# Reordering the opening of a windowed-attention and SwiGLU kernel: group 0's values between group 1's keys and queries, and a held first gate unit

## The chip, the cores and the metric

The kernel runs on one core of a Trainium2 chip. The metric is device time in microseconds (us), the median of several executions; lower is better. The engines of a core work side by side, each through its own list of instructions in order: TensorE (PE, matmuls, with its weight loads as PEld), VectorE (DVE), ScalarE (ACT), GpSimd (POOL, which here mostly issues the loads) and SyncE (SP, which issues the stores and the transposing transfers). They wait for each other through semaphores.

## The reference

Attention over 4 batches, 8 heads, 768 positions and head size 64. Each query sees the 128 latest keys up to itself, and the first 4 keys (the sinks). The outputs of the 8 heads stand side by side as one row of 512 per token, and go through a SwiGLU block without biases:

```
scores = scale * q @ k.T ; keep = is_sink | in_window
a = softmax(where(keep, scores, -1e9)) ; attn = a @ v
x = attn.transpose(0, 2, 1, 3).reshape(B * S, H * D)      # 3072 x 512
g = x @ w_gate ; val = x @ w_val                           # 512 x 1536 each
out = (g * sigmoid(g) * val) @ w_out                       # 1536 x 512
```

Inputs and outputs are float32; the kernel works in bfloat16 with float32 sums.

## The kernel before

The 3072 tokens are cut into 12 groups of 256 (three to a batch, `NG`), and attention is done group by group. The block is done in token tiles (`SIZES`): tiles 0, 1 and 2 of 256 tokens are groups 0, 1 and 2; larger tiles follow. The order of all work is written out by hand (`tc.manual_schedule()`): each engine gets its instructions in the order in which the Python code calls them, and nothing is moved by a scheduler.

The steps of attention, each with its line:

- `load_rows` (L95), `load_nat` (L104), `load_v` (L116), `load_gate` (L128), `load_out` (L137) issue loads on POOL's queue. Each issue there takes POOL's time, and POOL's queue lands them in the order of their issue. Keys and queries of group 1 come as `rows`, in two halves each of keys and of queries; the values of a group come as `va`, two halves.
- `step_T` (L220) turns keys or queries of group 1 so that the head size lies on the partitions: 16 matmuls of 64x64 for a half (`p2`) into one bank of PSUM, then one cast to `kT` or `qT` (L235). `step_TN` (L239) does it for later groups from another layout, with 4 transposes.
- `step_S` (L277): scores of 4 heads, 12 matmuls into 4 banks (L292), 4 exps on ACT (L299), and two mask products on DVE (L304). The masks are not issued there but appended to the list `later`; `flush` (L210) issues what the list holds.
- `step_ks` (L262), `step_K` (L308) and `step_vsb` (L268) make the sinks' keys, scores (`pk`, `es`) and values (`vsb`, made on POOL from `diag_h`, which three small DVE rows L602 to L604 compute).
- `step_PV` (L338): values of 4 heads of 128 tokens. In groups other than a batch's first, the first call starts all four `o` banks with the sinks (L335). Then a reciprocal (L363) and the scaled `xn`: by DVE in one row (L369), through `later`, or, with `norm` "a", by ACT in four rows (L366), at once.
- `step_X` (L379): four transposes of `xn` into the `px` bank (L396) and one copy to `xT`, the block's input, by ACT (L399) or DVE (L403), the latter through `later` or at once (`evict` "now").

A unit of the block is `gate` (L448): `gate_a` has `project` (L411) make the gate half `pg` in one bank, and ACT its tanh `th` (L432); then come the unit's attention steps; then `gate_b` makes the value half `pv`, and DVE gates in two rows, `u` (L438) and `ht` (L444). For a 256-token tile each half is 8 matmuls of 128x256. `both` (L455) does two units as gate half, gate half, value half, value half. `down` (L462) multiplies by `w_out`, scales and stores.

All PSUM tiles come from one pool of 8 banks, `bank` (L78), used in turn: a tile waits until the tile eight before it has been read.

The opening: group 0 comes pair by pair (`pair_T`, `pair_S`, `pair_mask`). L614 to L633 then interleave group 1's turning, group 0's values, transposes and group 1's scores. From L640 the list `us` holds the units in their order, and `weave` (L513) calls them, each with the attention steps that the slots (L654) give to its place: place 0 is unit (0, 0) of tile 0, place 1 is unit (0, 2) with group 1's values between its halves, place 2 is group 1's transposes alone, place 3 is units (0, 4) and (1, 0) through `both`, places 4 and 5 are units (1, 2) and (1, 4) with the turning of group 2. From place 6 on the units cover tiles 0 and 1 together, 512 tokens wide.

Of the kernel before, what the change touches and what calls it, by code (L numbers as in the profile page):

```python
# [14 lines left out]
def kernel(  # L15
# [12 lines left out]
    nc = tc.nc  # L28
# [55 lines left out]
    def by_rows(src, b, w, pairs, t0):  # L84

        hs = slice(2 * pairs.start + w, 2 * pairs.stop, 2)
        return src[b, hs, t0:t0 + 256].rearrange("p (m r) d -> m p (r d)", r=4)
# [3 lines left out]
    def new_rows(g):  # L91
        rows[g] = rowp.tile([P, 2, NP2, 4 * D], BF16, tag="rows", name="rows")
        return rows[g]

    def load_rows(g):  # L95
        b, c = divmod(g, GC)
        x = new_rows(g)
        for i in range(2):
            for w in range(2):
                nc.gpsimd.dma_start(  # L100
                    x[64 * w:64 * (w + 1), i],
                    by_rows((k, q)[i], b, w, ALL, c * 256))

    def load_nat(g):  # L104
        b, c = divmod(g, GC)
# [10 lines left out]
    def load_v(g):  # L116
        b, c = divmod(g, GC)
        va = vpool.tile([P, 2, H, VS], BF16, tag=f"va{g}", name="va")
        nc.vector.memset(va[:, :, :, D:D + 1], 1.0)  # L119
        for j in range(2):  # L120
            t0 = c * 256 + j * P
            nc.gpsimd.dma_start(  # L122
                va[:, j, :, 0:D], v[b, :, t0:t0 + P].rearrange("h p d -> p h d"))
        vas[g] = va
# [62 lines left out]
    for i in range(2):  # L187
# [2 lines left out]
                   allow_small_or_imprecise_dtypes=True)  # L190
    nc.gpsimd.iota(tk, [[0, 1]], base=0, channel_multiplier=1,
                   allow_small_or_imprecise_dtypes=True)
    load_rows(1)
    load_v(0)
    nc.gpsimd.iota(th8, [[-32, 4], [-NS, 4]], base=0, channel_multiplier=1,
                   allow_small_or_imprecise_dtypes=True)
    load_gate(0)
# [12 lines left out]
    def flush():  # L210
        for f in later:
            f()
        later.clear()
# [48 lines left out]
    def step_ks(b):  # L262
        for h in range(2):
            r = slice(h * D, (h + 1) * D)
            (nc.vector.tensor_copy if b else nc.scalar.copy)(
                out=kss[r, b, :, h * NS:(h + 1) * NS], in_=kTs[b][r, :, 0:NS])
# [144 lines left out]
    def project(ws, tb, f, name):  # L411
        n = xTs[tb].shape[2]
        ps = bank([P, 512], FP32, name)
        for i in range(512 // n):
            fi, fo = FOF[f + i]
            for c in range(DMC):
                nc.tensor.matmul(  # L417
                    ps[:, i * n:(i + 1) * n], ws[fi][:, c, fo * P:(fo + 1) * P],
                    xTs[tb][:, c], start=(c == 0), stop=(c == DMC - 1))
        return ps  # L420

    def gate_a(tb, f):
        if tb not in hts:
            n = SIZES[tb]
            t = hpool.tile([P, DFC * 512], BF16, tag="ht", name="ht")
            hts[tb] = dense(t, DFC, n)
            if tb == 0:
                hts["01"] = t.rearrange("p (b c n) -> p b c n", b=2, c=DFC)
                hts[1] = t[:, DFC * n:2 * DFC * n].rearrange("p (c n) -> p c n", c=DFC)
        pg = project(wgs, tb, f, "pg")  # L430
        th = tpool.tile([P, 512], FP32, tag="th", name="th")
        nc.scalar.activation(th, pg, AF.Tanh, scale=0.5)  # L432
        return pg, th

    def gate_b(tb, f, pg, th):
        pv = project(wvs, tb, f, "pv")
        u = upool.tile([P, 512], BF16, tag="u", name="u")
        nc.vector.scalar_tensor_tensor(u, th, 1.0, pg, op0=ALU.add, op1=ALU.mult)  # L438
        if tb == "01":
            nc.vector.tensor_tensor(  # L440
                hts[tb][:, :, f], *(x.rearrange("p (b n) -> p b n", b=2) for x in (u, pv)),
                op=ALU.mult)
            return
        nc.vector.tensor_tensor(  # L444
            hts[tb][:, f:f + 512 // SIZES[tb]].rearrange("p a n -> p (a n)"), u, pv,
            op=ALU.mult)
# [5 lines left out]
        gate_b(tb, f, *a)  # L452
        flush()

    def both(one_, two_, attn):  # L455

        a = [gate_a(*x) for x in (one_, two_)]
        for x, y in zip((one_, two_), a):
            gate_b(*x, *y)
        flush()  # L460

    def down(tb, ts, attn, last=False):  # L462
        at = {}
# [5 lines left out]
        for m, (lo, hi) in enumerate(parts):  # L469
# [11 lines left out]
            else:  # L481
                nc.vector.tensor_scalar(ot, po, 0.5, None, op0=ALU.mult)  # L482
            nc.sync.dma_start(out[r0:r0 + P, lo:hi], ot)

    def alone(tb, f, attn):
        pro(*attn)
        flush()

    def gates(tb):
        return [(gate, tb, f) for f in range(0, DFC, 512 // SIZES[tb])]  # L490
# [4 lines left out]
    def A(fn, *a):  # L495
        return lambda: fn(*a)

    def TN(g, evict="av"):
        return [A(step_TN, g, i, j, evict) for j in range(2) for i in range(2)]

    def Ss(g):
        return [A(step_S, g, p2) for p2 in range(2)]
# [7 lines left out]
    def K(g):  # L510
        return A(step_K, g)

    def weave(us, slots):  # L513
        assert all(i < len(us) for i in slots)
        for i, (fn, tb, x) in enumerate(us):
            fn(tb, x, slots.get(i, []))

    def pro(*steps):
        for s in steps:
            s()  # L520
            if len(later) > 1:
                later.pop(0)()

    def slots(*pairs):
        sl = {}
# [49 lines left out]
    def pair_mask(p):  # L575
        e = e_t[0][:, 2 * p:2 * p + 2, P:512]
        m = mask0.rearrange("q (o a) x -> q o (a x)", o=1)[:, :, P:512]
        nc.vector.tensor_tensor(e, e, m.broadcast_to([P, 2, 384]), op=ALU.mult)
# [20 lines left out]
    pair_S(3, 2)  # L599
    for p in range(1, NP2):  # L600
        pair_mask(p)
    nc.vector.tensor_scalar(lt8, th8, float(NS), None, op0=ALU.is_lt)  # L602
    nc.vector.scalar_tensor_tensor(lt8, th8, 0.0, lt8, op0=ALU.is_ge, op1=ALU.mult)
    nc.vector.tensor_reduce(diag_h, lt8.rearrange("p q h -> p h q"), mybir.AxisListType.X,  # L604
# [6 lines left out]
    load_gate(5)  # L611
    for i in range(4):
        load_out(i)
    step_T(1, 0, 0, "a")  # L614
    step_T(1, 0, 1, "a")
    step_T(1, 1, 0, "a")
    step_PV(0, 0, 0)
    step_PV(0, 0, 1)
    flush()
    step_T(1, 1, 1, "a")  # L620
    step_ks(0)
    step_PV(0, 1, 0)
    step_PV(0, 1, 1)
    flush()
    step_S(1, 0)
    masks1 = list(later)
    later.clear()
    step_X(0, 0)
    step_X(0, 1)
    flush()  # L630
    step_S(1, 1)
    later[:0] = masks1
    flush()  # L633
    load_nat(3)
    load_v(3)
    nc.gpsimd.memset(vcl, 0.0)
# [1 line left out]
    load_sinks(vcl, 1, B)  # L638

    g0, g1, g2 = gates(0), gates(1), gates(2)  # L640
    us = [g0[0], g0[1], (alone, 0, 0), (both, g0[2][1:], g1[0][1:]), g1[1],
          g1[2], *((gate, "01", f) for f in range(6, DFC)),
          *g2, *downs(0), *downs(1), *downs(2)]

    def L(*fs):
# [5 lines left out]
    def NV(g):  # L651
        return L(A(load_nat, g), A(load_v, g))

    weave(us, slots(  # L654
        (0, [K(1)]), (1, [A(step_PV, 1, 0, 0), A(step_PV, 1, 0, 1, "a"), A(step_PV, 1, 1, 0),
                              A(step_PV, 1, 1, 1, "a"), flush]),
        (2, [A(step_X, 1, 0, "a"), A(step_X, 1, 1, "now")]),
        ((4, 4, 5, 5), TN(2)), ((6, 7), Ss(2)), (6, [K(2)]),
        ((8, 8), PVs(2)[:2]), (9, [A(step_PV, 2, 0, 1, "a"), A(step_PV, 2, 1, 1, "a")]),
        ((10, 11), [A(step_X, 2, 0, "a"), A(step_X, 2, 1, "a")]),  # L660
        (11, [NV(4), lambda: nc.gpsimd.tensor_copy(out=vcl[64:128], in_=vcl[0:64])]), ((14, 14, 15, 15), TN(3, "aa")),
        (15, [A(xbar, 4)]), (15, [NV(5)]), (19, [A(xbar, 5)]), (19, [NV(6)]),
        (23, [A(xbar, 6)]), (23, [NV(7)]),
        ((17, 18), Ss(3)), (18, [A(step_ks, 1)]), (18, [A(step_vsb, 1)]),
# [59 lines left out]
```

## Time and profile before

| what | before |
|---|---|
| median of 4 runs | 239.22 us (238.61 to 239.97) |
| the profiled execution | 238.98 us, of which the span from first to last instruction is 237.2 us |
| granted TensorE clock, mean over the span | 0.999 |
| busy PE / DVE / ACT / POOL | 231.3 / 158.2 / 114.6 / 74.5 us |
| first gate half (`pg`) starts | 14.89 us |
| first 512-wide unit starts | 29.46 us |

All times within a profile are microseconds from the start of the span. A row of the timeline gives start, length, engine, line, operation, output and inputs, shapes, number of instructions, and in square brackets the idle time of the engine before it with what ended it. A length runs from the first start to the last end of the merged instructions, so that rows of a pipelined engine overlap by about 0.2 us on PE. A wait for several semaphores is put down to the one that came last. The digits of the 40 slices are tenths of busy share. The issue rows of POOL tell when a load is issued, not when its data land; landings are told separately.

In the stretch from 9 to 23 us the other engines' rows that matter for the change are these (start, length; engine, line and output; number):

```profile
12.35 0.59 ACT L235 CAST qT<-pt 128x512 bf16<-128x512 f32 x1 [0.73 <-PE pt L230]
12.83 0.41 ACT L265 COPY kss<-kT 64x16 bf16<-64x16 bf16 x2
13.27 4.03 ACT L299 ACTIVATE e<-s 128x512 bf16<-128x512 f32 x8
...
19.54 1.75 ACT L366 ACTIVATE xn<-o,rcp 128x64 bf16<-128x64 f32 x8 [0.90 <-DVE rcp L363]
21.13 0.64 ACT L399 COPY xT<-px 128x512 bf16<-128x512 bf16 x1
```

### The profile page before, as it was taken

Reading aid. Unit: us, or ns where it says so; the run is one execution under the profiler, and the core shown is the slowest. Engines: PE = TensorE matmul, PEld = TensorE weight load, DVE = VectorE, ACT = ScalarE, POOL = GpSimd, SP = SyncE. Lnnn points to the kernel's source line nnn. Section 1 sums busy time; section 2 is a strip of 40 time slices with the busy share of each in tenths; the row PEclk is TensorE's granted clock in tenths of the full one; section 3 lists DMA queues with packets and bytes.
Section 4 is the critical chain, followed back from the end, with each engine's and each line's share of the span. In section 5 each row is a group of like instructions: output and inputs, shape, how many; then the busy total and the mean of one; then the engine's idle time right before and its main releaser. Section 6 shows DMA issues by size and latency. Waiting matters only on the chain.

```text
span 237.2 us, 4913 instructions
## 1 busy us (share of the span) xinstructions
PE 231.3 (98%) x1901; PEld 127.7 (54%) x1901; DVE 158.2 (67%) x335; ACT 114.6 (48%) x237; POOL 74.5 (31%) x98
## 2 busy tenths in 40 slices
PE   8899999999999999999999999999999999999994
PEld 5577845795554444544444444444444445488443
DVE  5888778768652888960798980688970598877000
ACT  4896485467452836512845622655622663333221
POOL 8996875713508026170261700080000000000000
PEclk9999999999999999999999999999999999999999
DMA  8999999994999959999499994599214100200132
GB/s 139 157 182 177 181 200 205 157 148 75 158 170 153 164 107 118 143 121 220 112 115 123 109 79 147 137 88 140 44 21 140 63 3 0 44 3 1 52 128 88
DMA packets 107655, 27.36 MB, mean 115 GB/s; under 512 B 94704, under 2 KB 104688, under 8 KB 107632
## 3 DMA queue, kind: packets, MB, share of 16 engines
q0 software_dynamic: 76640, 13.90, 74.9%
q1 hardware_dynamic: 30448, 12.89, 25.4%
q8 instruction: 15, 0.25, 0.4%
q10 hardware_dynamic: 544, 0.26, 0.4%
q14 instruction: 8, 0.07, 0.1%
HBM read 28.34 MB, written 6.29 MB: 146 GB/s over the span
## 4 chain that ended last, share of the span: by engine, by line
PE 89%; ACT 4%; DVE 2%; DMA 2%; issue 1%; POOL 0%; DVEq 0%; ACTq 0%; POOLq 0%
PE pd L475 26%; PE pv L417 26%; PE pg L417 25%; PE o L355 4%; PE s L292 4%; DMA x<-in_q_dram 2%; ACT e L299 2%; PE pn L245 1%; ACT xn L366 1%; ACT e L572 1%; PE o L335 1%; ACT th L432 1%; PE pk L320 1%; DVE u L438 1%; PE px L396 0%
## 5 line engine op out<-in xcount | busy, mean ns | idle before, releaser
L438 DVE SCALAR_TENSOR_TENSOR u<-th,pg 128x512 bf16<-128x512 f32 x72 | 49.1, 683 | 38.9 <-ACT th L432 38.9
L417 PE MATMUL pv<-xT,wv 128*128 128x512 bf16 (+1 forms) x360 | 74.1, 337 | 0.3 <-ACT e L299 0.2
L417 PE MATMUL pg<-xT,wg 128*128 128x512 bf16 (+1 forms) x360 | 74.1, 336 | 0.2
L432 ACT ACTIVATE th<-pg 128x512 f32<-128x512 f32 x72 | 43.5, 604 | 62.3 <-PE pg L417 61.7
L475 PE MATMUL pd<-wo,ht 128*128 128x512 bf16 (+2 forms) x300 | 65.7, 371 | 0.0
L444 DVE TENSOR_TENSOR ht<-u,pv 128x512 bf16<-128x512 bf16 x66 | 45.4, 688 | 10.4 <-PE pv L417 4.5
L417 PEld LDWEIGHTS <-wg 128*128 128x128 bf16 x360 | 35.0, 98 | 28.1 <-issue 0.7
L299 ACT ACTIVATE e<-s 128x512 bf16<-128x512 f32 (+1 forms) x88 | 42.7, 581 | 3.5 <-PE s L292 3.5
L475 PEld LDWEIGHTS <-ht 128*128 128x128 bf16 x300 | 27.9, 98 | 30.0 <-issue 0.5
L417 PEld LDWEIGHTS <-wv 128*128 128x128 bf16 x360 | 32.0, 98 | 20.7 <-issue 1.6
L111 POOL DMA_DIRECT2D nat<-in_k_dram x20 | 17.6, 887 | 75.9 <-DMA qT<-nat 73.9
L480 ACT ACTIVATE ot<-pd 128x512 f32<-128x512 f32 (+1 forms) x24 | 14.3, 596 | 47.4 <-PE pd L475 47.4
L304 DVE TENSOR_TENSOR e<-e,mask 128x1024 bf16<-128x1024 bf16 (+1 forms) x44 | 27.2, 652 | 4.2 <-ACT e L299 4.2
L122 POOL DMA_DIRECT2D va<-in_v_dram x24 | 21.5, 917 | 4.7 <-DMA wo<-in_moe_w_out_dram 2.5
L369 DVE TENSOR_TENSOR xn<-o,rcp 128x256 bf16<-128x256 f32 x44 | 18.7, 424 | 1.5
L355 PEld LDWEIGHTS <-e 128*128 128x128 bf16 x352 | 15.0, 98 | 8.0 <-DVE va L119 0.5
L111 POOL DMA_DIRECT2D nat<-in_q_dram x20 | 17.7, 896 | 1.1 <-DMA wv<-in_moe_w_val_dram 0.5
L355 PE MATMUL o<-va,e 128*128 128x65 bf16 x352 | 17.0, 193 | 0.3 <-DVE va L119 0.3
L292 PE MATMUL s<-qT,kT 64*128 64x128 bf16 (+1 forms) x240 | 12.9, 237 | 0.0
L292 PEld LDWEIGHTS <-kT 64*128 64x128 bf16 x240 | 7.7, 94 | 7.6 <-issue 6.6
L482 DVE TENSOR_SCALAR ot<-pd 128x128 f32<-128x128 f32 x1 | 0.3, 292 | 14.3 <-PE pd L475 14.3
L363 DVE RECIPROCAL rcp<-o 128x4 f32<-128x4 f32 x48 | 8.1, 174 | 1.6 <-PE o L355 1.4
(73 smaller groups left out, 93.3 us busy)
## 6 DMA issues: line engine op xcount, KB each, us to landing
out_dram<-ot SPq DMA_DIRECT2D x23, 256.0 KB
va<-in_v_dram POOLq DMA_DIRECT2D x24, 128.0 KB, 6.5
nat<-in_k_dram POOLq DMA_DIRECT2D x20, 128.0 KB, 4.9
nat<-in_q_dram POOLq DMA_DIRECT2D x20, 128.0 KB, 5.8
wg<-in_moe_w_gate_dram POOLq DMA_DIRECT2D x6, 256.0 KB, 7.8
wv<-in_moe_w_val_dram POOLq DMA_DIRECT2D x6, 256.0 KB, 8.1
wo<-in_moe_w_out_dram POOLq DMA_DIRECT2D x4, 384.0 KB, 10.9
st<-in_q_dram ACTq DMA_DIRECT2D x2, 128.0 KB
```

Of the source, the lines that this page charges most:

```text
L111: nc.gpsimd.dma_start(x[:, i, j].rearrange("p (h d) -> p h d", d=D), src[b, :, t0:t0 + P].rearrange("h p d -> p h d"))
L122: nc.gpsimd.dma_start(va[:, j, :, 0:D], v[b, :, t0:t0 + P].rearrange("h p d -> p h d"))
L292: nc.tensor.matmul(pss[2 * pp + h][:, col:col + n], kTs[b][r, p, kk:kk + P], qTs[b][r, p, qq:qq + n], start=True, stop=True)
L299: nc.scalar.activation(e_t[g][:, h0 + h, lo:512], pss[2 * pp + h][:, lo:512], AF.Exp, scale=scale)
L304: nc.vector.tensor_tensor(e, e, m[:, :, lo:512].broadcast_to([P, 2, 512 - lo]), op=ALU.mult)
L355: nc.tensor.matmul(o, l, r, start=(c == 0 and i == 0), stop=(i == len(mms) - 1), skip_group_check=True)
L369: nc.vector.tensor_tensor(xn, po[:, :, 0:D], rcp.broadcast_to([P, 4, D]), op=ALU.mult)
L417: nc.tensor.matmul(ps[:, i * n:(i + 1) * n], ws[fi][:, c, fo * P:(fo + 1) * P], xTs[tb][:, c], start=(c == 0), stop=(c == DMC - 1))
L432: nc.scalar.activation(th, pg, AF.Tanh, scale=0.5)
L438: nc.vector.scalar_tensor_tensor(u, th, 1.0, pg, op0=ALU.add, op1=ALU.mult)
L444: nc.vector.tensor_tensor(hts[tb][:, f:f + 512 // SIZES[tb]].rearrange("p a n -> p (a n)"), u, pv, op=ALU.mult)
L475: nc.tensor.matmul(po, hts[tb][:, f, ts * P:(ts + 1) * P], wos[f // n][:, f % n, lo:hi], start=(f == 0), stop=(f == DFC - 1))
```

## The change

Loads: `load_rows` takes the tensor as an argument (0 keys, 1 queries), and group 0's values are issued between group 1's keys and queries instead of behind them. The three DVE rows for `diag_h`, `step_vsb` and the loads behind it are called after group 0's transposes instead of before group 1's turning.

Opening: group 1's keys are turned; then group 0's values (heads 4 to 7 of its first 128 tokens scaled by ACT); then group 1's queries; then the sinks' keys, transposes of group 0's first 128 tokens, scores (1, 0), transposes of the second 128 tokens. Both copies to `xT` are issued at once on DVE.

Units: `both`, `alone` and `pro` go. `gate_held` is unit (0, 0): gate half, then `step_K(1)`, scores (1, 1) and all four masks of group 1, then the value half; its tanh and gating rows are not issued but held. `gate_first` is unit (0, 2): gate half, group 1's values (heads 0 to 3 of both halves by ACT, heads 4 to 7 by DVE), the held tanh, its own tanh, transposes (1, 0), its value half, transposes (1, 1), then the gating of both units. Then the order is (1, 0), (1, 2), (0, 4), (1, 4); group 2's two key steps stand in place 4 and its two query steps in place 5.

```
@@ -92,14 +92,14 @@
...
 
-    def load_rows(g):
-        b, c = divmod(g, GC)
-        x = new_rows(g)
-        for i in range(2):
-            for w in range(2):
-                nc.gpsimd.dma_start(
-                    x[64 * w:64 * (w + 1), i],
-                    by_rows((k, q)[i], b, w, ALL, c * 256))
+    def load_rows(g, i):
+        b, c = divmod(g, GC)
+        if g not in rows:
+            new_rows(g)
+        for w in range(2):
+            nc.gpsimd.dma_start(
+                rows[g][64 * w:64 * (w + 1), i],
+                by_rows((k, q)[i], b, w, ALL, c * 256))
 
...
@@ -190,8 +190,9 @@
...
                    allow_small_or_imprecise_dtypes=True)
-    load_rows(1)
+    load_rows(1, 0)
     load_v(0)
+    load_rows(1, 1)
     nc.gpsimd.iota(th8, [[-32, 4], [-NS, 4]], base=0, channel_multiplier=1,
...
@@ -420,6 +421,10 @@
...
     def gate_a(tb, f):
+        new_h(tb)
+        return tanh(project(wgs, tb, f, "pg"))
+
+    def new_h(tb):
         if tb not in hts:
...
@@ -427,13 +432,16 @@
...
                 hts[1] = t[:, DFC * n:2 * DFC * n].rearrange("p (c n) -> p c n", c=DFC)
-        pg = project(wgs, tb, f, "pg")
+
+    def tanh(pg):
         th = tpool.tile([P, 512], FP32, tag="th", name="th")
...
     def gate_b(tb, f, pg, th):
-        pv = project(wvs, tb, f, "pv")
+        gate_v(tb, f, pg, th, project(wvs, tb, f, "pv"))
+
+    def gate_v(tb, f, pg, th, pv):
         u = upool.tile([P, 512], BF16, tag="u", name="u")
...
@@ -452,12 +460,31 @@
...
 
-    def both(one_, two_, attn):
-
-        a = [gate_a(*x) for x in (one_, two_)]
-        for x, y in zip((one_, two_), a):
-            gate_b(*x, *y)
+    held = []
+
+    def gate_held(tb, f, attn):
+
+        new_h(tb)
+        pg = project(wgs, tb, f, "pg")
+        for step in attn:
+            step()
+        pv = project(wvs, tb, f, "pv")
+        held.extend([lambda: held.append(A(gate_v, tb, f, *tanh(pg), pv))])
+
+    def gate_first(tb, f, attn):
+
+        pg = project(wgs, tb, f, "pg")
+        for hh, norm in ((0, "a"), (1, "v")):
+            for j in range(2):
+                step_PV(1, j, hh, norm)
         flush()
+        held.pop(0)()
+        a = tanh(pg)
+        step_X(1, 0, "now")
+        pv = project(wvs, tb, f, "pv")
+        step_X(1, 1, "now")
+        held.pop(0)()
+        gate_v(tb, f, *a, pv)
 
...
@@ -482,10 +509,6 @@
...
 
-    def alone(tb, f, attn):
-        pro(*attn)
-        flush()
-
     def gates(tb):
...
@@ -514,12 +537,6 @@
...
             fn(tb, x, slots.get(i, []))
-
-    def pro(*steps):
-        for s in steps:
-            s()
-            if len(later) > 1:
-                later.pop(0)()
 
...
@@ -599,6 +616,20 @@
...
         pair_mask(p)
+    step_T(1, 0, 0, "a")
+    step_T(1, 0, 1, "a")
+    step_PV(0, 0, 0)
+    flush()
+    step_PV(0, 0, 1, "a")
+    step_PV(0, 1, 0)
+    step_PV(0, 1, 1)
+    flush()
+    step_T(1, 1, 0, "a")
+    step_T(1, 1, 1, "a")
+    step_ks(0)
+    step_X(0, 0, "now")
+    step_S(1, 0)
+    step_X(0, 1, "now")
     nc.vector.tensor_scalar(lt8, th8, float(NS), None, op0=ALU.is_lt)
...
@@ -611,26 +642,6 @@
...
         load_out(i)
-    step_T(1, 0, 0, "a")
-    step_T(1, 0, 1, "a")
-    step_T(1, 1, 0, "a")
-    step_PV(0, 0, 0)
-    step_PV(0, 0, 1)
-    flush()
-    step_T(1, 1, 1, "a")
-    step_ks(0)
-    step_PV(0, 1, 0)
-    step_PV(0, 1, 1)
-    flush()
-    step_S(1, 0)
-    masks1 = list(later)
-    later.clear()
-    step_X(0, 0)
-    step_X(0, 1)
-    flush()
-    step_S(1, 1)
-    later[:0] = masks1
-    flush()
     load_nat(3)
...
@@ -638,8 +649,8 @@
...
     g0, g1, g2 = gates(0), gates(1), gates(2)
-    us = [g0[0], g0[1], (alone, 0, 0), (both, g0[2][1:], g1[0][1:]), g1[1],
-          g1[2], *((gate, "01", f) for f in range(6, DFC)),
+    us = [(gate_held, *g0[0][1:]), (gate_first, *g0[1][1:]), g1[0], g1[1], g0[2], g1[2],
+          *((gate, "01", f) for f in range(6, DFC)),
           *g2, *downs(0), *downs(1), *downs(2)]
...
@@ -652,13 +663,12 @@
...
     weave(us, slots(
-        (0, [K(1)]), (1, [A(step_PV, 1, 0, 0), A(step_PV, 1, 0, 1, "a"), A(step_PV, 1, 1, 0),
-                              A(step_PV, 1, 1, 1, "a"), flush]),
-        (2, [A(step_X, 1, 0, "a"), A(step_X, 1, 1, "now")]),
-        ((4, 4, 5, 5), TN(2)), ((6, 7), Ss(2)), (6, [K(2)]),
+        (0, [K(1), A(step_S, 1, 1), flush]),
+        (4, TN(2)[::2]), (5, TN(2)[1::2]), ((6, 7), Ss(2)), (6, [K(2)]),
         ((8, 8), PVs(2)[:2]), (9, [A(step_PV, 2, 0, 1, "a"), A(step_PV, 2, 1, 1, "a")]),
         ((10, 11), [A(step_X, 2, 0, "a"), A(step_X, 2, 1, "a")]),
-        (11, [NV(4), lambda: nc.gpsimd.tensor_copy(out=vcl[64:128], in_=vcl[0:64])]), ((14, 14, 15, 15), TN(3, "aa")),
+        (11, [NV(4), lambda: nc.gpsimd.tensor_copy(out=vcl[64:128], in_=vcl[0:64])]),
+        ((14, 14, 15, 15), TN(3, "aa")),
         (15, [A(xbar, 4)]), (15, [NV(5)]), (19, [A(xbar, 5)]), (19, [NV(6)]),
...
```

## The prediction

> **What bounds the kernel now.** I read the page first: the engines' shares and the 40 slices.
>
> ```profile
> PE 231.3 (98%) x1901; PEld 127.7 (54%) x1901; DVE 158.2 (67%) x335; ACT 114.6 (48%) x237; POOL 74.5 (31%) x98
> ...
> PE   8899999999999999999999999999999999999994
> ...
> PEclk9999999999999999999999999999999999999999
> ```
>
> TensorE (PE) is the bound and has 5.9 us without work in a span of 237.2. Next, busy time by stretches, to see where those 5.9 us lie (columns: stretch, its length, then busy us of each engine with its instructions, the granted clock, DMA share, GB/s).
>
> ```profile
> 10.00:20.00 10.00, 9.16 (x163) 7.02 (x162) 8.68 (x26) 8.06 (x20) 9.45 (x13) 1.00 1.67 181
> ...
> 30.00:60.00 30.00, 29.87 (x274) 19.11 (x272) 23.52 (x47) 19.33 (x44) 15.18 (x21) 1.00 1.55 156
> 60.00:100.00 40.00, 39.90 (x341) 19.65 (x340) 28.36 (x61) 20.60 (x42) 13.15 (x16) 1.00 1.40 146
> ...
> 150.00:200.00 50.00, 50.00 (x366) 23.86 (x365) 36.55 (x70) 24.30 (x49) 5.25 (x6) 1.00 0.51 71
> ```
>
> From 30 us on PE never lacks work for long, so a delay made in the opening is carried to the end, and a gain too. The edit changes no arithmetic: it can only close or open holes on PE before 30 us. So I read PE's rows of the opening in order of time (start, length, group, idle time before it and what ended that).
>
> ```profile
> 8.80 1.24 PE L230 MATMUL pt<-ident,rows 64*64 64x64 bf16 x33
> 10.37 0.63 PE L230 MATMUL pt<-ident,rows 64*64 64x64 bf16 x15 [0.32 <-DMA rows<-in_q_dram]
> 11.34 0.40 PE L355 MATMUL o<-va,e 128*128 128x65 bf16 x8 [0.34 <-DVE va L119]
> ...
> 14.89 1.03 PE L417 MATMUL pg<-xT,wg 128*128 128x256 bf16 x8
> ...
> 20.25 0.92 PE L396 MATMUL px<-ident,xn 128*128 128x128 bf16 x7
> 21.35 0.23 PE L396 MATMUL px<-ident,xn 128*128 128x128 bf16 x1 [0.18 <-ACT xn L366]
> ...
> 21.42 2.07 PE L417 MATMUL pg<-xT,wg 128*128 128x256 bf16 x16
> ```
>
> What to see: PE waits for group 1's query rows at 10.37, for group 0's values at 11.34 (the row names a memset on VectorE, but it ends at 11.31 by chance; the values' first half had landed at 11.20). At 21.42 one row holds 16 matmuls: 8 are unit (0,4)'s gate half, which needs nothing new, and only the next 8, from 22.45, need group 1's turned output. Work stands ready where the last copy of xT is waited for.
>
> The loads that set the first two waits, on GpSimd's (POOL's) queue:
>
> ```profile
> 4.47 1.27 POOL L100 DMA_DIRECT2D rows<-in_q_dram  x2
> 5.68 1.85 POOL L122 DMA_DIRECT2D va<-in_v_dram  x2
> ```
>
> The landing marks give key rows 8.27 and 8.92, query rows 9.59 and 10.32, values 11.20 and 11.99: half a row load adds 0.65 to 0.73 us to the line, half a value load 0.79 to 0.88.
>
> **The change, part by part.** The order is fixed by hand, so what the new source says is what each engine gets. I walk it forward from 8.80 us: an instruction starts when its engine is free and what it waits for has ended, about 0.05 us later on PE and 0.03 elsewhere. Prices, start to start, from rows of the opening: 8 matmuls of a gate half 0.875 us; 16 of a turn of rows 0.48; 12 of scores 0.44; 8 value matmuls 0.24; 4 transposes 0.22; about 0.1 where PE changes its tile shape; about 0.2 from a matmul's start to its result. ScalarE: cast 0.59, exp 0.48 apart, scaling of one head 0.2 apart. VectorE: reciprocal 0.17, xn 0.42, copy of xT 0.42, mask 0.69, the three lt/diag rows with the memsets together 0.8.
>
> 1. *Values before query rows on POOL's queue.* By the steps above, after 8.92 the values land at 9.8 and 10.6, the queries at 11.3 and 12.05. Bounds for the second query half: 10.3 if the value packets cost the queue nothing, 12.6 if a value half takes 5.5 us from issue (as in this trace) and the queries queue up behind both. I take 12.05, since the total moved up to then was 11.99 before. SP's queue and the later loads keep their order.
>
> 2. *Group 0's values between keys and queries.* Keys end on PE at 9.9. Heads 0 to 3 go at 10.0, heads 4 to 7 at 10.52 (the last mask ends at 10.48), the other 16 matmuls from 10.65 to 11.1. Before, they ended at 12.7. Moving part of xn to ScalarE (11.16 to 12.11) costs nothing: ScalarE would wait for the queries there. But PE then waits until 12.1 for the queries, turns them until 13.1, and transposes xn's first half at 13.13. The first scores need the first query cast (12.80 to 13.39), so they run 13.45 to 13.95. The second half of xn goes at 14.02, its copy runs 14.48 to 14.91, and the first gate half starts at 14.96. Before it started at 14.89. The earlier values win nothing there, because the chain query rows, cast, scores, second transpose, copy runs from the delayed landing.
>
> 3. *Scores (1,1) behind the first gate half.* At 14.89 the kernel before had both score sets of group 1 done; now the second set follows at 16.10 to 16.54, so 0.44 plus two shape changes, some 0.6 us, are still owed. It waits on no bank: its four wait for a copy and three exps that end by 15.5.
>
> 4. *Held unit, values behind the second gate half.* PE runs without a hole from 14.96 to 20.0: gate half, sinks' scores 15.93, scores, value half to 17.50, second gate half to 18.37, sinks 18.46, 32 value matmuls 18.8 to 20.0. ScalarE's last exp ends at 18.57, the last mask at 19.29, when PE reaches its heads at about 19.3: just covered, and a late exp is paid one to one. Then reciprocals 19.24 onward and ScalarE's eight scalings from 19.45 to 21.23. VectorE's xn of heads 4 to 7 end at 20.36 and 20.91. Transposes (1,0) finish at 20.6 (0.35 us of hole), the value half fills 20.66 to 21.54, transposes (1,1) go right behind. The held tanh is queued on ScalarE behind the scalings and both gating pairs on VectorE behind the copies; who waits for them is PE, for banks, at 26.9, when the bank has been free since 23.8: nothing.
>
> 5. *Unit (1,0) directly after.* The copy of transposes (1,1) runs 22.00 to 22.43, and PE stands from 21.77 to 22.48: here the old order had unit (0,4)'s gate half as cover, and the new one has none. Unit (1,0) starts at 22.48 against 22.45 in the trace, but with one gate half, 0.875 us, less behind it.
>
> 6. *Group 2's keys in one unit, queries in the next; lt8 rows after the xT copies.* The same transposes in other pairs: nothing. vsb moves from 14.28 to 15.7 and the group-2 loads, issued behind it, from 14.85 to about 16.3; they stand in a queue whose line lands them at 23.2 and later, and PE wants the keys at 26.9 and the queries at 29.1: nothing, at worst (1.4 us later, 26.8) still nothing.
>
> The sum: from 22.48, eight gate or value halves (7.0) and 16 transposes (0.89) reach the first 512-wide unit at 30.36. The same count for before, seven halves from 22.45, gives 29.46, which is what the trace has. So +0.9 us. The profiled execution took 238.98 (span 237.2 and 1.8 around it), and the sum is 239.9 on it; that execution lies 0.24 below the median 239.22, so for a median I say 240.1: slower by 0.4%, within the 0.5% (1.2 us) that this kernel's runs can tell from no change.
>
> **A rule weighed.** Row first: PEclk is 9 in every slice, and the 14 filling matmuls at the start lie 0.21 us apart where a gate half's, equally wide, lie 0.109 apart later. The Trainium skill ("TensorE: Matmul & The Clock Gate", Part 1) says that the clock falls to half after an idle window of about 3.4 us. It speaks against holes such as the new one at 11.1 to 12.1, but by its figure no hole of the walk is long enough and the sum stays; were it to fall, my estimate from the page is 1.7 us for one window.
>
> **Rivals.**
> - *Not slower: the swap costs the queries nothing.* If they land by about 11 us, item 2's chain starts at the end of the values, the first gate half at 14.1, and 0.85 of the 0.9 us is won back: 239.2. For it: transfers of one queue overlap in flight (issue to landing 5.1 us against 0.6 us between landings). Against: six landings one behind the other, at the pace of their sizes. It decides once the second half lands before 11.1.
> - *Later queries or masks.* Landing at 12.6 puts 0.55 on top, the exps late by 0.3 another 0.3: 240.6 to 241.0. For it: item 4 has no slack; against: the walk over the old order came out 0.05 to 0.1 us from the trace.
> - *The clock.* With PE thinner from 10 to 12 us a slow stretch as at the start (matmuls at twice the distance for the 3.7 us between the first filling matmul and 4.75, where the record of the clock begins) would cost 1.85: 242.0. Against: before idles 0.6 and 0.5 us in the same stretch at full clock.
>
> **How the numbers follow.** The walk 0.63 (own range 239.6 to 240.7), queries not late 0.12, later 0.17, clock 0.05, something faster that I do not see 0.03. The range runs from 238.9 (queries not late, less the runs' scatter) to 241.4 (later ones, plus it). Slower by over 0.5% means above 240.4: a third of the walk, most of the later ones, the clock: 0.40. Faster by over 0.5%: 0.03. The rest, 0.57, lies within.
>
> **What the next profile would show.** Values on PE at 10.0 and a wait there for query rows ending near 12.1; first gate half near 15.0; scores between the first gate half and its value half; PE idle some 0.7 us before unit (1,0), released by the copy of xT; the first 512-wide unit near 30.4 against 29.46. The prediction is wrong if the query rows land near 10.5, if PE's hole before unit (1,0) is short, or if the stretch from 30 us to the end changes its length.

## The result and the profile after

The changed kernel takes 240.01 us in the median (239.37 to 241.65 in 38 executions) against 239.31 us for the kernel before, run beside it: a ratio of 1.0028 with a 95% interval of 1.0017 to 1.0038, so 0.4 to 0.9 us slower, 0.67 in the middle (the medians lie 0.70 apart). The profiled execution took 239.67 us with a span of 237.9 (before: 238.98 and 237.2). I read it in the order in which the prediction read the profile before. First the page: busy time of the engines, the slices and the granted clock.

```profile
PE 231.0 (97%) x1901; PEld 127.8 (54%) x1901; DVE 158.0 (66%) x335; ACT 114.9 (48%) x240; POOL 74.9 (31%) x98
...
PE   7898999999999999999999999999999999999994
...
PEclk9999999999999999999999999999999999999999
```

The work is the same, the clock is the same, and TensorE (PE) has 6.9 us without work where it had 5.9. Then busy time by stretches (stretch, its length, busy us of PE, PEld, DVE, ACT and POOL with their instructions, granted clock, DMA share, GB/s).

```profile
10.00:20.00 10.00, 9.02 (x177) 7.06 (x171) 7.52 (x25) 8.78 (x25) 8.76 (x12) 1.00 1.56 176
20.00:25.00 5.00, 4.30 (x42) 3.68 (x42) 4.23 (x10) 2.65 (x9) 3.67 (x5) 1.00 2.12 169
...
30.00:60.00 30.00, 29.87 (x271) 19.19 (x270) 23.75 (x45) 19.27 (x44) 15.45 (x21) 1.00 1.54 156
...
150.00:200.00 50.00, 50.00 (x368) 23.82 (x367) 35.96 (x69) 24.73 (x50) 5.25 (x6) 1.00 0.52 72
```

From 30 us on, PE's busy time is that of before to the hundredth in these stretches (29.87 and 50.00): what was lost was lost earlier. The stretch from 20 to 25 us has 4.30 busy where the kernel before had 4.82:

```profile
20.00:25.00 5.00, 4.82 (x44) 3.71 (x43) 3.54 (x8) 2.96 (x10) 3.17 (x5) 1.00 2.11 168
```

PE's rows of the opening show where (start, length, group, and in brackets the idle time before it with what ended it).

```profile
9.46 1.08 PE L231 MATMUL pt<-ident,rows 64*64 64x64 bf16 x32
10.48 0.35 PE L356 MATMUL o<-va,e 128*128 128x65 bf16 x6
11.20 0.72 PE L356 MATMUL o<-va,e 128*128 128x65 bf16 x18 [0.36 <-DVE e L595]
11.85 1.23 PE L231 MATMUL pt<-ident,rows 64*64 64x64 bf16 x32
...
14.80 1.03 PE L418 MATMUL pg<-xT,wg 128*128 128x256 bf16 x8 [0.52 <-DVE xT L404]
...
15.99 0.61 PE L293 MATMUL s<-qT,kT 64*128 64x128 bf16 x12
...
20.32 0.34 PE L397 MATMUL px<-ident,xn 128*128 128x128 bf16 x3 [0.18 <-ACT xn L367]
20.50 1.04 PE L418 MATMUL pv<-xT,wv 128*128 128x256 bf16 x8
21.37 0.39 PE L397 MATMUL px<-ident,xn 128*128 128x128 bf16 x4
22.27 1.03 PE L418 MATMUL pg<-xT,wg 128*128 128x256 bf16 x8 [0.52 <-DVE xT L404]
...
30.15 1.03 PE L418 MATMUL pg<-xT,wg 128*128 128x512 bf16 x4
```

Two holes of 0.52 us are new, both ended by a copy to xT (L404): one ahead of the first gate half, one ahead of unit (1, 0) at 22.27. Before, a single row of 16 gate matmuls stood over the second. The first 512-wide unit starts at 30.15 against 29.46, 0.69 later, which is the difference of the two spans. That an opening's loss arrives whole at the end holds for nearly every profile of this study: from the first 512-wide unit to the end of the span it is 207.74 to 207.78 us in twelve of the thirteen, and 209.12 in one of the better versions below. The list of PE's waits between 7 and 32 us sums it up (line, waited for, us in total, times, longest):

```profile
PE pg L418 <- DVE xT L404: 1.0, 2, 0.5
PE o L356 <- DVE e L595: 0.4, 1, 0.4
```

Two more of 0.2 each follow. The same list of the kernel before has four waits of 0.3, 0.3, 0.2 and 0.2, some 1.0 us in all against 1.8 here; its two longest are those for the values and for the query rows, as the prediction read them:

```profile
PE o L355 <- DVE va L119: 0.3, 1, 0.3
PE pt L230 <- DMA rows<-in_q_dram: 0.3, 1, 0.3
```

In this profile of the changed kernel the waits for loads are gone, and waits for VectorE came in their place. The loads of POOL's queue:

```profile
3.23 1.28 POOL L100 DMA_DIRECT2D rows<-in_k_dram  x2
4.47 1.83 POOL L122 DMA_DIRECT2D va<-in_v_dram  x2
6.29 1.26 POOL L100 DMA_DIRECT2D rows<-in_q_dram  x2
```

Their landing marks are 9.24 and 10.24 for the values, 11.07 and 11.95 for the queries (predicted 9.8, 10.6, 11.3, 12.05). PE does not show a wait for the queries in this execution, because group 0's staged loads landed late (ScalarE waited for the last of them until 5.62; before, until 4.65), the keys' turn began at 9.46 instead of 8.80, and PE came to the queries only at 11.85. That start is not the change's doing: over all the profiles of this study it lies between 8.60 and 9.71 us, whatever the kernel (last section).

### The profile page after: what moved, and what is told of

The parts are those of the page before. It is cut to its first block, busy times and chain, and to the rows that moved or that the text cites. A ratio compares the mean times of both kernels' runs of the same rounds, so it can differ in the third digit from the quotient of the medians.

```text
span 237.9 us, 4912 instructions
## 1 busy us (share of the span) xinstructions
PE 231.0 (97%) x1901; PEld 127.8 (54%) x1901; DVE 158.0 (66%) x335; ACT 114.9 (48%) x240; POOL 74.9 (31%) x98
## 4 chain that ended last, share of the span: by engine, by line
PE 90%; ACT 3%; DVE 2%; DMA 2%; issue 1%; ACTq 0%; DVEq 0%
PE pd L502 26%; PE pv L418 26%; PE pg L418 26%; PE s L293 4%; PE o L356 4%; DMA st<-in_q_dram 2%; ACT e L300 1%; PE px L397 1%; PE pn L246 1%; ACT e L589 1%; PE pk L321 1%; PE o L336 1%; ACT th L438 1%; PE pt L231 0%; ACT xn L367 0%
## 5 line engine op out<-in xcount | busy, mean ns | idle before, releaser
L502 PEld LDWEIGHTS <-ht 128*128 128x128 bf16 x300 | 27.9, 98 | 29.9 <-issue 0.5
L370 DVE TENSOR_TENSOR xn<-o,rcp 128x256 bf16<-128x256 f32 x43 | 18.2, 424 | 1.5
## 6 DMA issues: line engine op xcount, KB each, us to landing
wo<-in_moe_w_out_dram POOLq DMA_DIRECT2D x4, 384.0 KB, 11.1
```

The lines of the kernel that those rows point to most:

```text
L370: nc.vector.tensor_tensor(xn, po[:, :, 0:D], rcp.broadcast_to([P, 4, D]), op=ALU.mult)
L502: nc.tensor.matmul(po, hts[tb][:, f, ts * P:(ts + 1) * P], wos[f // n][:, f % n, lo:hi], start=(f == 0), stop=(f == DFC - 1))
```

## The experiments

The theory: unit (1, 0) has lost its cover, the gate half of unit (0, 4), and that is the main loss. The rivals: the later landing of the query rows is the main loss; the held tanh and gating rows are. Each of the kernels below computes the whole reference. Since the start of an opening wanders, I use two measures beside the ratio: the time from the last of the six loads (key rows, query rows, values) to the first 512-wide unit, and the time from group 0's first transposes (px), or the first gate half, to that unit.

**The cover put back.** Unit (0, 4) goes through `both` with (1, 0) again; all else as after.

```
-    us = [(gate_held, ...), (gate_first, ...), g1[0], g1[1], g0[2], g1[2],
+    us = [(gate_held, ...), (gate_first, ...), (nothing, 0, 0),
+          (both, g0[2][1:], g1[0][1:]), g1[1], g1[2],
```

> The changed kernel with one thing put back: unit (0,4)'s gate half stands again between group 1's last transposes and unit (1,0)'s gate half (the two units as gate half, gate half, value half, value half). Theory A (the walk on record: the loss is the missing cover for the last copy of xT): the hole before unit (1,0), 0.5 us in the profile of the changed kernel, is filled, the first 512-wide unit starts at 29.5 to 29.6 instead of 30.15, time about 239.4 to 239.5, ratio to before 1.000 to 1.001. Rival B (the loss is the later landing of the query rows): it stays at 30.1, ratio 1.003. Rival C (the loss is the held gating, crowding VectorE and ScalarE behind the copies): it stays at 30.1 or a wait for a bank shows up, ratio 1.003 or more.

Measured: 239.30 us against 239.14, ratio 1.0006 [0.9983, 1.0030]. PE's rows:

```profile
14.25 1.03 PE L418 MATMUL pg<-xT,wg 128*128 128x256 bf16 x8 [0.52 <-DVE xT L404]
...
20.96 0.39 PE L397 MATMUL px<-ident,xn 128*128 128x128 bf16 x4
21.31 1.92 PE L418 MATMUL pg<-xT,wg 128*128 128x256 bf16 x16
23.54 1.92 PE L418 MATMUL pv<-xT,wv 128*128 128x256 bf16 x16 [0.31 <-DMA wv<-in_moe_w_val_dram]
...
29.68 1.03 PE L418 MATMUL pg<-xT,wg 128*128 128x512 bf16 x4
```

The hole before unit (1, 0) is gone: from the second transposes (px) to the next gate half it is 0.35 us (20.96 to 21.31) where it was 0.90 (21.37 to 22.27), and from the first gate half to unit (1, 0)'s place it is 7.06 us instead of 7.47. But the covering unit needs the third chunk of `wv`, which lands at 23.49, and PE now stands there: the values begin 0.48 us after the 16 gate matmuls would have ended (21.31 plus two halves of 0.875 is 23.06). From the first gate half to the wide unit it is 15.43 us against 15.35 after, so in this execution the gain was paid back. Measured against the kernel before, the time is 0.5 us better than the whole change's, with intervals that overlap. The cover is a real part of the loss; this run alone does not give its size.

**The old load order, the rest as after.**

```
-    load_v(0)
     load_rows(1, 1)
+    load_v(0)
```

> The changed kernel with the loads in the old order (group 1's queries issued ahead of group 0's values), PE's order unchanged. A: the queries still stand behind the values on PE, and the values now land near 12.0, so everything behind shifts by 0.5 to 0.6 us: first gate half at 15.3 to 15.5, first 512-wide unit at 30.7 to 30.8, ratio 1.005 to 1.006. B: the queries land at 10.3 again and the loss goes: 29.5, ratio 1.000. C: as the changed kernel, 1.003.

Measured: 240.15 us against 239.14, 1.0041 [1.0021, 1.0062]. The queries landed at 9.03 and 10.03, and the first 512-wide unit came at 30.33 (I expected 30.7 to 30.8). This profile cannot judge the loads: as in the first one of after, PE shows no wait for a load in its opening, and the unit's 0.18 us go with a start of the keys' turn that was 0.25 later (9.71). The times can: taking the swap back wins nothing, so the later landing of the query rows is not what the whole change costs.

**The new units alone**, on the loads and the opening of before (scores (1, 1) behind the first gate half, `gate_held`, `gate_first`, then (1, 0), (1, 2), (0, 4), (1, 4)).

```
-    us = [g0[0], g0[1], (alone, 0, 0), (both, g0[2][1:], g1[0][1:]), g1[1], ...
+    us = [(gate_held, ...), (gate_first, ...), g1[0], g1[1], g0[2], g1[2], ...
```

> The kernel before (its loads, its turning and values of the opening, its transposes) with only the new units: scores (1,1) and all masks behind the first gate half, the held unit, unit (1,0) without cover. A: the units alone cost nearly all: 0.6 to 0.8 us, first 512-wide unit at 30.1 to 30.2, ratio 1.0025 to 1.0035. B: nothing, 29.5, ratio 1.000. C: as A.

Measured: 240.01 us, 1.0035 [1.0018, 1.0053]. Both new holes are there, 0.52 us before the first gate half at 15.15 and 0.52 before unit (1, 0) at 22.62, and the wide unit comes at 30.50 (expected 30.1 to 30.2; the keys' turn began at 9.70 here). The units alone cost as much as the whole change.

**The new opening alone**, on the units of before, with scores (1, 1) right behind the second transposes.

```
+    step_X(0, 0, "now")
+    step_S(1, 0)
+    step_X(0, 1, "now")
...
     step_S(1, 1)
     flush()
```

> The kernel before with the new loads and the new opening (values between keys and queries, transposes around scores (1,0)), scores (1,1) and the masks called right behind the second transposes, and the old units with their cover. A: the copy of the second transposes, waited for at 14.3 to 14.8 in the changed kernel, is covered by the scores, but the eight exps start 0.6 to 0.8 us later than before, and the masks and the old unit (0,2) wait for them: 0.4 to 0.7 us, first 512-wide unit at 29.9 to 30.1, ratio 1.0015 to 1.003. B: all of the loss, 30.15, ratio 1.003. C: nothing, 29.5, ratio 1.000.

Measured: 239.56 us, 1.0023 [1.0011, 1.0035].

```profile
11.48 0.24 PE L231 MATMUL pt<-ident,rows 64*64 64x64 bf16 x1 [0.38 <-DMA rows<-in_q_dram]
12.14 1.08 PE L231 MATMUL pt<-ident,rows 64*64 64x64 bf16 x31 [0.42 <-DMA rows<-in_q_dram]
...
18.95 0.29 PE L336 MATMUL o<-vsb,es 32*128 32x260 bf16 x4 [0.49 <-ACT es L325]
```

Here the query rows do bind, for 0.80 us, and the sinks' exp (`es`), queued on ScalarE behind eight exps, holds PE 0.49 more. The wide unit came at 30.41, later than the expected 29.9 to 30.1. So the opening has a price of its own, and the two parts (0.35% and 0.23%) do not add up to the whole (0.28%).

**The kernel before and the kernel after, unchanged, once more**, for the scatter of the openings.

> The kernel before, unchanged, for a second profile. The profiles so far start the turning of group 1's keys anywhere from 8.65 to 9.71 us, with no order by kernel: the second staging transfer of group 0 lands between 4.2 and 5.5 us. New theory D: the kernel before is held by its loads (queries 10.3, values 11.2 to 12.0) and not by that start, so its first 512-wide unit starts at 29.4 to 29.6 whether the keys are turned at 8.8 or at 9.5. Rival: the start decides, and the first 512-wide unit moves with it one to one (30.1 for 9.5).

> The changed kernel, unchanged, for a second profile and its time beside the next two. D: it is held by whichever is later, the start or the query rows. If the keys are turned at 8.7 to 9.0, PE waits for the queries at 11.1 to 12.0 as the prediction had it, and the first 512-wide unit still starts at 30.1 to 30.3; if they are turned at 9.4 or later there is no such wait and the time goes up with the start, 20.7 us after it. Ratio to before 1.0028 again. Rival: with an early start it comes at 29.5 to 29.7, so that the two kernels differ only by luck of the start.

The single execution of before fell on a late load (last section), took 244.06 us and decides nothing here. The kernel after: 239.58 us against 239.06, 1.0018 [0.9999, 1.0037]. Its profile began early, with the keys' turn at 8.78, and it shows what the first one hid:

```profile
11.16 0.62 PE L356 MATMUL o<-va,e 128*128 128x65 bf16 x15 [0.39 <-DMA va<-in_v_dram]
...
12.54 1.08 PE L231 MATMUL pt<-ident,rows 64*64 64x64 bf16 x31 [0.46 <-DMA rows<-in_q_dram]
...
15.34 1.03 PE L418 MATMUL pg<-xT,wg 128*128 128x256 bf16 x8 [0.52 <-DVE xT L404]
...
22.81 1.03 PE L418 MATMUL pg<-xT,wg 128*128 128x256 bf16 x8 [0.52 <-DVE xT L404]
...
30.69 0.38 PE L418 MATMUL pg<-xT,wg 128*128 128x512 bf16 x1
```

The second value half landed at 11.12 and the second query half at 12.49, and an early start won nothing: PE waited 0.46 us for the queries, and the wide unit came at 30.69, later than the 30.1 to 30.3 expected for such a start, since the queries landed later than the expected 11.1 to 12.0. From px to the wide unit it is 17.14 us, as in the first profile (13.01 to 30.15): in these two the tail behind the query rows is the same, and the beginning is set by whichever of PE and the landing is later.

**Scores (1, 1) in the first hole**, behind the second transposes, the rest as after.

```
     step_X(0, 1, "now")
+    step_S(1, 1)
...
-        (0, [K(1), A(step_S, 1, 1), flush]),
+        (0, [K(1), flush]),
```

> The changed kernel with scores (1,1) moved from behind the first gate half to behind the second transposes of group 0, into the hole of 0.52 us before the first gate half. A: the 0.44 us of scores fit the hole, but their exps now stand ahead of the sinks' exp on ScalarE, and the sinks' matmuls wait for it: 0.2 to 0.4 us gained of 0.5, ratio to before 1.0012 to 1.002. Rival: the exps are late anyway and the masks decide, no gain, 1.0028.

Measured: 239.70 us, 1.0020 [1.0004, 1.0036]; px at 13.23, the wide unit at 30.25, so 17.02 us instead of 17.14: 0.12 of the 0.2 to 0.4 that I expected, and nothing in the medians (239.58 for the kernel after beside it).

```profile
14.44 0.88 PE L293 MATMUL s<-qT,kT 64*128 64x128 bf16 x12
```

The scores take 0.88 us there instead of 0.61 (in the next kernel the same matmuls show a wait of 0.28 us for an exp), so the hole is filled and the gate half, at 15.43, starts later than the copy would let it.

**Both holes filled**: as the last, with the sinks' scores ahead of scores (1, 1), the cover put back, and in `both` the value half of (1, 0) ahead of that of (0, 4), so that the third chunk of `wv` is wanted later.

```
+    step_K(1)
+    step_S(1, 1)
...
+        for x, y in ((two_, a[1]), (one_, a[0])):
+            gate_b(*x, *y)
```

> The changed kernel with both holes filled: the sinks' scores and scores (1,1) behind the second transposes of group 0, unit (0,4)'s gate half ahead of unit (1,0)'s, and the value half of (1,0) ahead of that of (0,4), whose weights land near 23 us. A: the two gains add, 1.0 to 1.1 us less than the changed kernel: 238.9 to 239.0, ratio to before 0.998 to 0.9995. Rival: filled holes are dug elsewhere by the exps and masks behind them, ratio 1.000 to 1.001 as with the cover alone.

Measured: 238.91 us, 1.0000 [0.9982, 1.0019] (expected 0.998 to 0.9995), 0.67 below the kernel after and 0.79 below the last one on the same chip.

```profile
21.89 1.91 PE L418 MATMUL pg<-xT,wg 128*128 128x256 bf16 x16
23.64 1.91 PE L418 MATMUL pv<-xT,wv 128*128 128x256 bf16 x16
```

No hole and no wait for `wv`. From px (13.51) to the wide unit (29.77) it is 16.26 us, 0.76 less than with only the first hole filled, as the medians say. This is the size that the first experiment could not show. Three things differ from the last kernel, but the rows tell them apart: from the second transposes to the next gate half it is 0.22 us (21.67 to 21.89) instead of 0.90 (21.47 to 22.37), so 0.68 of the 0.76 lie at the cover. With its weights in time, the cover is worth the whole loss.

**The load swap alone**, on the kernel before.

```
+    load_rows(1, 0)
     load_v(0)
+    load_rows(1, 1)
```

> The kernel before with only the loads swapped (group 0's values issued ahead of group 1's queries), PE's order unchanged. Theory D (the query rows land 1.3 to 2 us later with the swap, at 11.4 to 12.5, and that is paid wherever they are wanted early): here PE wants them at 10 us, ahead of the values, so the opening waits for them and the first 512-wide unit comes 0.8 to 1.3 us later than 29.46, ratio to before 1.004 to 1.0055. Rival: the two loads change places at no cost, since the values are then there when the queries are done: ratio 1.000 to 1.001.

Measured: 240.13 us against 239.24, 1.0051 [1.0031, 1.0070], 6 executions. PE's waits before 32 us name one load for nearly all of it:

```profile
PE pt L231 <- DMA rows<-in_q_dram: 1.6, 2, 1.1
```

With PE's old order, which wants the queries first, the swap costs 0.9 us between the medians and 1.2 by the ratio. With PE's new order it costs nothing that shows (1.0028 with the swap, 1.0041 without it), but the intervals overlap, so that it gains anything there is not shown. (The profiled execution also had a lower clock, see the last section, and its wide unit came at 31.73, beyond the expected range; the other five, at 1.000, have a median of 240.11.)

**Better versions.** First the loads and opening of before, with the held unit, the split transposes (1, 0) and (1, 1) around its value half, and the cover; then the same with the two edits of the both-holes kernel:

```
+    step_K(1)
     step_S(1, 1)
...
-        for x, y in zip((one_, two_), a):
+        for x, y in ((two_, a[1]), (one_, a[0])):
```

> The loads and the opening of the kernel before with scores (1,1) in their old place, the held unit and its split transposes from the changed kernel, and unit (0,4)'s gate half as cover ahead of unit (1,0). A with D (what is lost are the cover and the later queries, what the held unit gains is the value half between the two transposes): 0.3 to 0.4 us faster than before, first 512-wide unit at 29.0 to 29.2, ratio 0.998 to 0.999. Rival: the held gating costs what the split saves, ratio 1.000.

> As e10, with the sinks' scores ahead of scores (1,1) and the value half of unit (1,0) ahead of that of (0,4), whose weights land at 22.3 to 23.5 us in the runs so far. A with D: as e10 where those weights land by 22.8, up to 0.3 us better where they land later: ratio 0.9975 to 0.999. Rival: no difference from e10 or a loss, since the sinks' exp then delays the exps of scores (1,1).

Measured: 239.28 us, 1.0000 [0.9979, 1.0021], and 238.94 us, 0.9982 [0.9967, 0.9997], against 239.24. The first, expected at 0.998 to 0.999, gained nothing in its times. In its profile it reached its wide unit at 28.88, the earliest of all, and then lost time where the kernel before lost none:

```profile
112.32 1.02 PE L418 MATMUL pg<-xT,wg 128*128 128x512 bf16 x4 [0.88 <-DMA xT<-xn]
```

Whether that wait for a transposing transfer comes of the order or of the execution, one profile cannot tell. (The third chunk of `wv`, which the expectation of the second has at 22.3 to 23.5, landed between 21.50 and 23.49 in all profiles but the repeated one of before.) The second has its wide unit 17.21 us behind the last of the six landings (11.91 to 29.12) against 17.47 in the kernel before (11.99 to 29.46), 17.40 in the first, 17.31 with both holes filled and 18.20 in the kernel after. It is ahead of the kernel before by 0.3 us in the medians and 0.4 by the ratio, and its interval only just leaves out no change; from the interval of the kernel after, 1.0017 to 1.0038, it is well clear.

## Why the prediction was right, and where its terms were off

The forecast was +0.9 us from lost cover, slower by 0.4%. The mechanism stands, and the size was 0.70 between the medians, 0.67 by the ratio and 0.69 in the profile. That the profile's landings and start fell so that the parts met the forecast this closely is partly luck (item 2).

1. *Load order.* Right: values 9.24 and 10.24, queries 11.07 and 11.95, the second halves within 0.4 and 0.1 us of the predicted ones. What the bounds did not say is that the last landing moves from 11.36 to 12.49 between the seven profiles with this order.
2. *PE waits for the queries until 12.1.* Right in kind, and shown where the start was early (0.46 us in the second profile of after). In the first profile PE itself was late by 0.66 us and the wait is not to be seen. "The earlier values win nothing" holds: the first gate half is at 14.80, predicted 14.96. But there the late start stood where the query wait was forecast, so that these two numbers lie so close is luck: the same opening has its first gate half at 14.25 with the queries landed at 11.36 (the cover put back) and at 15.34 with 12.49 (the second profile of after).
3. *Scores (1, 1) behind the first gate half.* At 15.99, predicted 16.10. The 0.6 us that I called owed are not simply won by moving them into the hole ahead: there they cost 0.88, and 0.12 was won.
4. *Held unit.* Right: no hole from 14.80 to the transposes, a short one there, value half at 20.50 (20.66). The last mask ends at 19.20 and PE goes on without a wait. The held rows cost nothing: ScalarE has both tanh rows done at 22.06, and no wait of PE names them or their banks.
5. *The cover gone.* Right, and the main term: the hole at 22.27 is released by L404. I had PE stand from 21.77 to 22.48, 0.71 us; the copy ran 21.79 to 22.21 and PE went on at 22.27. The row shows 0.52 us of idle time because it counts a matmul to its end; counted from start to start as in the prediction (four transposes 0.22 from 21.37), the hole is 0.68. So the price of the lost cover was right, and the place was 0.21 us early. 0.16 of them are the chain's start (14.80 for 14.96, and still 20.50 for 20.66 in item 4), the other 0.05 lie between transposes (1, 1) and the end of their copy. Unit (1, 0) thus came 0.18 ahead of before (22.45) with one half more behind it: 0.875 less 0.18 is the measured 0.69. The missed point was not in my walk at all: the cover depends on `wv`, and PE's own order decides whether the chunk has landed (in the trace of before it lands at 22.30, and PE comes to it at 23.33 or later).
6. *Group 2, vsb.* Right: vsb at 15.40 (15.7), the group-2 loads from 16.34 (16.3), no wait for them in PE's list.

The rival with queries not late (first gate half at 14.1) did not come about: the second half never landed before 11.36 with this order, and its limit was 11.1. It came near in the profile of the cover put back, where PE found the queries landed at 11.37 and the first gate half is at 14.25; over the six profiles with the new loads and the new opening PE waits 0.42 to 0.80 us for the queries in four, and not at all in two. The rival with later ones (12.6) came about in part: landings of 12.46 and 12.49 occur, and the profiled execution with 12.49 took 240.21. The clock rival did not show in any of the kernel after's executions (0.998 to 1.000 in all), but it did in others. What I held against it, that before idles 0.6 and 0.5 us from 10 to 12 at full clock, was misread: the two waits there are 0.32 and 0.34 us.

## What to carry to other kernels

Where an engine waits for a copy of its own last result, the unit that stands ready beside it is worth the length of the hole (0.68 us here); before an order is straightened, ask which row stood over which wait, and for the covering row also when its weights land. Two loads of one queue that swap places while their consumer keeps its order cost 0.9 to 1.2 us here; with the consumer's order swapped too, neither a cost nor a gain of the loads could be told. Compare openings from what releases them, a landing or the engine's own late start, and not from the start of the span: the wide unit of the two profiles of the kernel after lies 0.54 us apart (30.15 and 30.69) by that alone.

## What the runs showed of the hardware

*Landings scatter by about 1 us, and now and then by more.* The second half of group 0's queries (`x`, on POOL's queue) was issued at 2.12 or 2.13 us in all thirteen profiles and landed between 6.58 and 7.58. With values ahead of queries the second value half, issued between 5.37 and 5.41, landed between 9.99 and 11.12. In the repeated profile of before, that load, issued at 6.58 instead of 6.59, landed at 15.20 instead of 11.99:

```profile
15.24 0.98 PE L355 MATMUL o<-va,e 128*128 128x65 bf16 x15 [2.92 <-DMA va<-in_v_dram]
```

*The clock fell after a hole shorter than I had taken to be needed.* The record of the granted clock changes only in steps of 3.41 us after its first entry: in that execution of the kernel before it is full from 4.16 to 14.40 us (three steps) and half from 14.40 to 21.22 (two), and with only the loads swapped full from 5.38 to 12.21 (two) and half from 12.21 to 15.62 (one). So I took the busy time by these stretches (columns as above; the granted clock is the third number from the end). The repeated run of the kernel before:

```profile
10.98:14.40 3.42, 1.11 (x26) 0.90 (x26) 1.40 (x7) 1.47 (x4) 2.19 (x3) 1.00 1.34 171
14.40:17.81 3.41, 2.57 (x34) 2.11 (x34) 1.16 (x5) 1.01 (x3) 2.20 (x4) 0.50 1.87 177
17.81:21.22 3.41, 3.41 (x33) 1.87 (x30) 3.06 (x6) 3.25 (x8) 3.41 (x5) 0.50 1.62 189
```

The kernel with only the loads swapped:

```profile
8.79:12.21 3.42, 1.78 (x51) 1.48 (x48) 2.43 (x8) 2.04 (x5) 3.42 (x5) 1.00 1.53 164
12.21:15.62 3.41, 3.41 (x59) 2.78 (x53) 2.12 (x8) 1.56 (x5) 3.28 (x6) 0.50 1.47 180
15.62:19.03 3.41, 3.32 (x47) 2.38 (x44) 2.59 (x6) 3.41 (x8) 3.24 (x5) 1.00 1.84 181
```

Here PE was never idle for more than 1.09 us at once, 1.64 us in two waits that lie 0.24 apart, and half the clock for 3.41 us is 1.7 us lost. The Trainium skill ("TensorE: Matmul & The Clock Gate", Part 1) has the clock fall after at least one idle window of about 3.4 us. The length agrees with the steps of this record; but the window before this fall had 1.78 us of work in it, so it need not be without work, and a hole need not be that long.

Nor does such a hole always bring it: the both-holes kernel idled for 0.36, 0.57 and 0.42 us between 9.9 and 12.5 us, and its clock stayed at 1.00. These holes fall into two of its stretches, and the emptier one still has 2.44 us of work:

```profile
8.41:11.82 3.41, 2.44 (x60) 1.85 (x59) 2.64 (x9) 3.11 (x10) 3.41 (x6) 1.00 1.40 152
```

Sorted in this way, all thirteen traces agree. The clock falls fifteen times in them, twice in an opening and thirteen times at the end, where PE's work stops, and each time after a stretch with at most 1.78 us of work. No stretch at full clock with 1.90 us or more was followed by a fall; the one with 1.90 is at the end of the first of the better versions, and the next ones have 2.3:

```profile
233.00:236.41 3.41, 1.90 (x20) 1.28 (x18) 0.29 (x1) 0.49 (x1) 0.00 (x0) 1.00 0.43 152
```

By these traces the limit lies between 1.78 and 1.90 us of PE's work, as the profile counts it, in a stretch of 3.41. So whether a hole costs the clock depends also on how it lies to the steps. That rests on one stretch on either side, and no run was made to try it. The clock came back after a stretch that PE had filled (3.41), and not after the one with 2.57 at half the clock.

Five of the experiments' executions had a mean clock of 0.986 to 0.993, and each was the slowest of its kernel, or its only one (240.68 to 244.06 us). Two of the five have a trace, the two shown.
